# Keys' weights turned in two halves, and the first two token tiles together, at the start of a linear-attention and Mish block

## The chip, the cores and the metric

The kernel runs on one core of one Trainium2 chip. The time is the device time of one execution in microseconds; it is the median of several. Before the change it is 173.72 us, the median of three executions between 173.6 and 174.08.

A core has a matrix engine (TensorE, PE in the profile; its weight loads are the row PEld), an elementwise and reduction engine (VectorE, DVE), an engine for functions and copies (ScalarE, ACT), GpSimd (POOL) and SyncE (SP), which here only issues transfers. Engines run side by side, each works through its own instructions in order, and they wait for each other by semaphores. ACT can issue transfers too. All transfers run on the core's 16 DMA engines.

## The reference

With x of 2048 tokens by 512 (bf16), xn is x normalised over its 512 values. The result is x plus an attention branch of xn plus a dense branch of xn.

```python
qkv = x @ wqkv                      # 32 heads of 16: q, k, v
pq = einsum("bhsd,hdf->bhsf", q, w_phi)
pk = einsum("bhsd,hdf->bhsf", k, w_phi)
phi_q = concatenate([softmax(pq), softmax(-pq)], -1)
phi_k = concatenate([softmax(pk), softmax(-pk)], -1)
kv = einsum("bhsf,bhsd->bhfd", phi_k, v)
z  = einsum("bhsf->bhf", phi_k)
o  = einsum("bhqf,bhfd->bhqd", phi_q, kv) / (einsum("bhqf,bhf->bhq", phi_q, z) + 1e-6)
A  = o.reshape(B, S, D) @ wo
h  = xn @ w1 + b1                   # 512 -> 1792
B  = (h * tanh(softplus(h))) @ w2   # Mish, 1792 -> 512
out = x + A + B
```

## The kernel before

The 2048 tokens are 16 tiles of 128, in four groups of four. All of x, of the turned normalised tokens (`xnT`) and of the activations lies in the core's memory. The logits of keys and queries are not computed in two products: the 16 by 16 matrices `w_phi` of the heads are laid out as blocks on a diagonal (`Wbd`, made by `weights_by_block`, L524, from the loaded `wsrc` and a mask), and the columns of `wqkv` for the keys are multiplied by them once ("folded") to give `wkp`. For this fold TensorE needs the keys' weights turned, `wT`, with `wT[p, j, r]` = row r, column 128 j + p of the keys' part. `load_turned` (L143) fetches it with a transposing DMA on the sync queue. The fold has four steps, one for each 128 rows of the weights (`F0 0` to `F0 3`, L156); step kt reads the columns 128 kt to 128 kt + 127 of `wT`'s last dimension, so steps 0 and 1 read rows 0 to 255 and steps 2 and 3 the rest. Each is copied to `wkp` by `FD` (L165). The queries' weights go the same way later, by `load_queries`.

Tiles 0 and 1 of the first group start by a path of their own, a tile at a time: statistics on VectorE (`LS`, L170 and L172), the inverse root on GpSimd (`RS`, L176 and L177), normalising on VectorE (`AZ`, L181), four transpositions on TensorE (`TP`, L560), and a copy to `xnT` (`TC`, L565). Then come the first logits (`LP`, L209): for each of the four row blocks of `wkp`, tile 0 and then tile 1. The values of tile 0 follow (`V 0`, L194, with weights `wv`), then tiles 2 and 3, then the rest: hidden layer (`H`, L228), Mish on ACT (`M`, L239), softmaxes (`E`, `X`, `S`, `R`, `N`), sums over keys (`A`), second layer (`O`, L463), output projection (`P`, L470), residual (`Y`, L477).

The order of all this is written out by hand in `STEPS`: it is the order in which each engine gets its instructions. A step that waits holds up everything behind it on its engine. The transfers at the start are issued ahead of the steps, in the order of the code from L483: the sync queue issues tile 0 of x, `wT`, tiles 2 and 3, `wv`, the first half of `w1`, tiles 4 to 7, the second half of `w1`; ACT issues `wsrc`, tile 1 of x and the bias `b1b`. Transfers signal on eight semaphores in turn, so a later transfer also waits for an earlier one on the same semaphore. TensorE's first work is 12 matmuls on constants (L513), whose result nothing uses.

Of the kernel before, what the change touches and what calls it, by code (L numbers as in the profile page):

```python
# [21 lines left out]

WARM = 12
STEPS = """
LS 0; RS 0; DX 2; LS 1; WB; RS 1; AZ 0; TP 0 @0; F0 0 @1; F0 1 @2; AZ 1; FD 0 v; TP 1 @3; TC 1 v; LS
2; PB @4; RS 2; TC 0 a; LS 3; RS 3; FD 1 a; AZ 2; F0 2 @5; F0 3 @0; FD 2 a; FD 3 a; LP i @1,2; KM;
DX 3; AZ 3; V 0 @3; LC 0 0 a; TP 2 @5; V 1 @0; TC 2 a; TP 3 @1; VC 0 a; LC 0 1 v; TC 3 v; CB; L 0 2
@5; L 0 3 @2; LC 0 3 a; LN 1; H 0 @3; H 1 @1; H 2 @4; M 0; LC 0 2 a; H 3 @2; M 1; M 2; M 3; VC 1 a;
# [34 lines left out]
def kernel(  # L63
# [12 lines left out]
    nc = tc.nc  # L76
    P = 128
    S, D, NH, DH, F = 2048, 512, 32, 16, 1792
# [4 lines left out]
    FT = F // P  # L83
# [3 lines left out]
    x_v = A_x.flatten_outer_dims().rearrange("(t p) d -> p t d", p=P)  # L87
# [19 lines left out]
    x_sb = persist.tile([P, NT, D], BF16, name="x_sb")  # L107
# [29 lines left out]
            tables[0] = name  # L137
            nc.scalar.preload_act_table_set(name)  # L138

    def load_turned(base_col):  # L140

        wT = lnp.tile([P, 4, 512], BF16, name="wT", tag="xn")
        nc.sync.dma_start_transpose(out=wT[:], in_=A_wqkv[:, base_col : base_col + D])  # L143
        return wT

    def bank(b, name, dtype=FP32):
# [333 lines left out]

    part = (slice(0, 384), slice(384, 512))

    nc.sync.dma_start(x_sb[:, 0, :], x_v[:, 0, :])  # L483
    wT_of = {0: load_turned(D)}
    with nc.allow_non_contiguous_dma(reason="tiny w_phi load"):
        nc.scalar.dma_start(wsrc[:], wphi_v)
    nc.scalar.dma_start(x_sb[:, 1, :], x_v[:, 1, :])
    nc.scalar.dma_start(b1b[:], b1_v[:, :])
    nc.sync.dma_start(x_sb[:, 2:4, :], x_v[:, 2:4, :])
    nc.sync.dma_start(wv[:], wqkv_v[:, :, 2 * D : 3 * D])  # L490
# [8 lines left out]
    for sign in (1, -1):  # L499
        nc.gpsimd.affine_select(  # L500
            out=block[:], in_=block[:], pattern=[[-16 * sign, 8], [0, 16]],
# [83 lines left out]

    def load_weights(i):
        if i == 2:
            for f in (slice(0, 5), slice(5, 10), slice(10, FT)):
                nc.sync.dma_start(w2_sb[:, f, :], w2_v[:, f, :])
        else:  # L590
            nc.sync.dma_start(wo_sb, wo_v[:, :, :])
# [6 lines left out]
        pl_of[1, i] = project(wkp, TPG + i, wide_of[0][:, i - 1, :])  # L598

    def load_queries():  # L600
        wT_of[1] = load_turned(0)

    run = {
        "KM": masks, "WB": weights_by_block, "PB": bias,
# [2 lines left out]
        "LP": first_logits, "TC": lambda i, c: first_keep(i, copies[c]),  # L607
        "F0": lambda kt, b: fold(wT_of[0], kt, b), "FD": lambda kt, c: unfold(wkp, kt, copies[c]),
        "LN": stats, "AP": apply, "DX": load_tokens, "DW": load_weights, "WL": wide,
        "L": logits, "LC": lambda s, i, c: take(s, i, copies[c]),  # L610
        "V": value, "VC": lambda t, c: keep(t, copies[c]),
# [6 lines left out]
        "PH": lambda h: project_out(NT - 1, part[h]),  # L618
        "YH": lambda h: residual(NT - 1, part[h], (nc.scalar, nc.sync)[h]),
        "WT": load_queries,  # L620
        "F": lambda kt, b: fold(wT_of[1], kt, b), "FC": lambda kt, c: unfold(wqp, kt, copies[c]),
    }
# [33 lines left out]
```

## Time and profile before

| | |
|---|---|
| median of three executions | 173.72 us |
| the profiled execution, its own time | 174.0 us |
| its span in the profile | 172.3 us |
| granted TensorE clock in it | 1.0 |
| TensorE busy | 168.7 us, 98% |
| VectorE busy | 143.2 us, 83% |
| ACT busy | 119.5 us, 69% |
| bytes moved by DMA | 18.02 MB, 105 GB/s in the mean |
| from issue to landing: tile 0 of x, tile 1 of x, wT, tiles 2 and 3, wv | 2.4, 3.1, 5.4, 3.2, 4.5 us |

How to read it: times are from the start of the span. A line of the timeline has the start, the length, the engine, the line of the kernel, the operation, output and inputs, and in brackets how long the engine had been idle and what released it. SPq and ACTq are the two engines' queues issuing transfers: the length there is the time to issue, not to land. A group that the timeline merges has the length from its first start to its last end. A wait line has who waited for what, the total, the number of times and the longest, in us.

### The profile page before, as it was taken

The numbers are of one execution on the slowest core, as the hardware profiler recorded it, in microseconds if no ns is written. First come the engines' busy times: TensorE is split into PE (matmuls) and PEld (weight loads), VectorE is DVE, ScalarE is ACT, GpSimd is POOL, SyncE is SP. The second block draws the span as 40 slices with busy tenths as digits, with TensorE's granted clock in tenths as the row PEclk, the third lists the DMA queues.
The fourth block names the chain that finished last, engine by engine and source line by source line (L and its number), as shares of the span: only waits on it lengthen the run. The fifth ranks groups of instructions, "written<-read, shape, count | busy, mean of one in ns | idle before, by whom it ended". The sixth has DMA issues, their size and how long they took to land.

```text
span 172.3 us, 2713 instructions
## 1 busy us (share of the span) xinstructions
PE 168.7 (98%) x1039; PEld 82.4 (48%) x1039; DVE 143.2 (83%) x221; ACT 119.5 (69%) x192; POOL 9.4 (5%) x26
## 2 busy tenths in 40 slices
PE   8999999999999999999999999999999999999993
PEld 2554444444545444454446544444444545445452
DVE  2878998999997999979999999799988996844433
ACT  2446889979899998989999988974063883414200
POOL 4332205000000000000000000000000000000000
PEclk9999999999999999999999999999999999999999
DMA  5999350199930000000000363023974749885641
GB/s 98 269 377 365 82 98 0 37 189 207 366 120 0 0 4 0 0 0 0 4 0 0 64 118 66 12 51 67 150 152 93 150 95 144 172 168 100 173 134 61
DMA packets 44953, 18.02 MB, mean 105 GB/s; under 512 B 37004, under 2 KB 44940, under 8 KB 44940
## 3 DMA queue, kind: packets, MB, share of 16 engines
q1 hardware_dynamic: 44096, 17.60, 44.5%
q10 hardware_dynamic: 844, 0.25, 0.6%
q8 instruction: 8, 0.13, 0.3%
q14 instruction: 5, 0.04, 0.1%
HBM read 6.84 MB, written 2.10 MB: 52 GB/s over the span
## 4 chain that ended last, share of the span: by engine, by line
PE 95%; DMA 3%; SPq 0%; DVE 0%; issue 0%
PE po L463 28%; PE ph L228 28%; PE pl L194 14%; PE po L470 8%; PE pv L194 8%; DMA wT<-in_A_wqkv_dram 3%; PE pnd L418 2%; PE pkv L387 2%; PE pfold L156 1%; PE pwide L194 1%; PE pl L209 1%; PE ptr L560 0%; SPq L483 0%; DVE x_sb L477 0%; PE pb L533 0%
## 5 line engine op out<-in xcount | busy, mean ns | idle before, releaser
L463 PE MATMUL po<-w_sb,acts 128*128 128x512 bf16 (+2 forms) x238 | 50.7, 366 | 0.0
L228 PE MATMUL ph<-xnT,w_sb 128*128 128x512 bf16 x224 | 50.1, 379 | 0.0
L239 ACT ACTIVATE acts<-ph,b1f 128x512 bf16<-128x512 f32 x56 | 37.2, 694 | 4.6 <-PE ph L228 4.4
L305 DVE TENSOR_REDUCE s<-e 128x128 f32<-128x2048 bf16 x16 | 36.4, 2279 | 2.5 <-ACT e L288 2.5
L228 PEld LDWEIGHTS <-w_sb 128*128 128x128 bf16 x224 | 21.7, 98 | 25.5
L463 PEld LDWEIGHTS <-acts 128*128 128x128 bf16 x238 | 22.3, 98 | 24.1
L288 ACT ACTIVATE e<-e 128x2048 bf16<-128x2048 bf16 x16 | 30.3, 1908 | 0.0
L194 PEld LDWEIGHTS <-xnT 128*128 128x128 bf16 x184 | 17.6, 98 | 20.1 <-DMA wv<-in_A_wqkv_dram 0.2
L252 ACT CAST p_sb<-pl 128x512 bf16<-128x512 f32 x27 | 15.4, 587 | 5.5 <-PE pl L194 4.7
L433 ACT COPY ds<-pnd 128x32 f32<-128x32 f32 x16 | 2.9, 183 | 23.5 <-PE pnd L418 23.5
L194 PE MATMUL pv<-wv,xnT 128*128 128x512 bf16 x64 | 16.1, 379 | 0.0
L477 DVE TENSOR_TENSOR x_sb<-po,x_sb 128x512 bf16<-128x512 f32 (+2 forms) x17 | 10.9, 654 | 5.7 <-PE po L470 5.7
L470 PE MATMUL po<-wqk,xnT 128*128 128x512 bf16 (+2 forms) x68 | 15.5, 366 | 0.0
L194 PE MATMUL pl<-wqk,xnT 128*128 128x512 bf16 x64 | 15.3, 379 | 0.0
L170 DVE BATCH_NORM_STATS2 stats<-x_sb 128x6 f32<-128x512 bf16 x16 | 10.1, 679 | 4.3 <-DMA x_sb<-in_A_x_dram 4.3
L263 DVE TENSOR_TENSOR m<-m 128x512 bf16<-128x512 bf16 (+1 forms) x32 | 11.5, 358 | 1.1
L194 PE MATMUL pl<-wkp,xnT 128*128 128x512 bf16 x48 | 11.7, 379 | 0.0
L263 DVE TENSOR_TENSOR m<-p_sb 128x1024 bf16<-128x1024 bf16 x16 | 10.9, 682 | 0.2 <-ACT p_sb L252 0.2
L272 DVE TENSOR_TENSOR e<-p_sb,m 128x2048 bf16<-128x2048 bf16 x8 | 9.8, 1226 | 1.4 <-PE pkv L387 1.1
L272 DVE TENSOR_TENSOR e<-m,p_sb 128x2048 bf16<-128x2048 bf16 x8 | 9.8, 1225 | 0.3
L340 DVE TENSOR_TENSOR e<-e,r 128x2048 bf16<-128x2048 bf16 x8 | 9.6, 1215 | 0.0
L138 ACT ACT_TABLE_LOAD x7 | 9.0, 1283 | 0.1
(62 smaller groups left out, 131.4 us busy)
## 6 DMA issues: line engine op xcount, KB each, us to landing
out_dram<-x_sb SPq DMA_DIRECT2D x15, 128.0 KB, 2.0
w_sb<-in_B_w_dram SPq DMA_DIRECT2D x2, 896.0 KB, 7.8
x_sb<-in_A_x_dram SPq DMA_DIRECT2D x3, 512.0 KB, 10.0
w_sb<-in_B_w_dram SPq DMA_DIRECT2D x2, 640.0 KB, 8.8
wv<-in_A_wqkv_dram SPq DMA_DIRECT2D x1, 512.0 KB, 4.5
wqk<-in_A_wo_dram SPq DMA_DIRECT2D x1, 512.0 KB, 4.6
w_sb<-in_B_w_dram SPq DMA_DIRECT2D x1, 512.0 KB, 9.6
x_sb<-in_A_x_dram SPq DMA_DIRECT2D x1, 256.0 KB, 3.2
```

What stands on the lines that cost most here:

```text
L170: nc.vector.bn_stats(stats[:, i, :], xs[:, i, :])
L194: nc.tensor.matmul(pp, lhsT=xnT[:, t, kt, :], rhs=w[:, kt, :], start=(kt == 0), stop=(kt == KT - 1),)
L228: nc.tensor.matmul(ph_of[u][:], lhsT=w1_sb[:, kt, f * P : (f + 1) * P], rhs=xnT[:, g * TPG : (g + 1) * TPG, kt, :], start=(kt == 0), stop= ...
L239: nc.scalar.activation(acts[:, f, g * 512 : (g + 1) * 512], ph_of.pop(u)[:], ACT.Mish, bias=b1f[:, f : f + 1])
L252: copy(p_of[s][:, i, :], pl_of.pop((s, i)))
L263: nc.vector.tensor_tensor(out=m[:], in0=src[:, :, 0:half], in1=src[:, :, half : 2 * half], op=op)
L272: nc.vector.tensor_tensor(out=e_of[s][:].rearrange("p t j l c -> p (t j) l c")[:, :, pl, :].rearrange("p t (c e o) -> p t c e o", e=8, o=2 ...
L288: nc.scalar.activation(v, v, ACT.Exp)
L305: nc.vector.reduce_sum(t[:], pair(s, k).rearrange("p t j l (c e) -> p (t j l c) e", e=16), axis=AX.X)
L463: nc.tensor.matmul(po_of[t, c.stop][:, c], lhsT=acts[:, f, t * P : (t + 1) * P], rhs=w2_sb[:, f, c], start=(f == 0), stop=False,)
L470: nc.tensor.matmul(po_of[t, c.stop][:, c], lhsT=oT_of[t // 2][:, t % 2 * 4 + j, :], rhs=wo_sb[:, j, c], start=False, stop=(j == 3),)
L477: nc.vector.tensor_tensor(out=y, in0=po_of.pop((t, c.stop))[:, c], in1=y, op=ALU.add)
```

## The change

Tile 1 of x moves from ACT's queue to the sync queue, right behind tile 0 and ahead of `wT`. `wT` is fetched by two transposing DMAs of 256 rows each instead of one of 512; the queries' weights are still fetched by one. The step `WB`, which makes the block weights on VectorE, moves ahead of the statistics of tile 1. `w2` is loaded in two pieces of 7 blocks instead of three of 5, 5 and 4.

```diff
-LS 0; RS 0; DX 2; LS 1; WB; RS 1; AZ 0; TP 0 @0; F0 0 @1; F0 1 @2; AZ 1; FD 0 v; TP 1 @3; TC 1 v; LS
+LS 0; RS 0; DX 2; WB; LS 1; RS 1; AZ 0; TP 0 @0; F0 0 @1; F0 1 @2; AZ 1; FD 0 v; TP 1 @3; TC 1 v; LS
...
-    def load_turned(base_col):
+    def load_turned(base_col, *rows):
 
         wT = lnp.tile([P, 4, 512], BF16, name="wT", tag="xn")
-        nc.sync.dma_start_transpose(out=wT[:], in_=A_wqkv[:, base_col : base_col + D])
+        for r in rows:
+            nc.sync.dma_start_transpose(out=wT[:, :, r], in_=A_wqkv[r, base_col : base_col + D])
         return wT
...
-    nc.sync.dma_start(x_sb[:, 0, :], x_v[:, 0, :])
-    wT_of = {0: load_turned(D)}
+    for t in range(2):
+        nc.sync.dma_start(x_sb[:, t, :], x_v[:, t, :])
+    wT_of = {0: load_turned(D, slice(0, 256), slice(256, 512))}
     with nc.allow_non_contiguous_dma(reason="tiny w_phi load"):
         nc.scalar.dma_start(wsrc[:], wphi_v)
-    nc.scalar.dma_start(x_sb[:, 1, :], x_v[:, 1, :])
     nc.scalar.dma_start(b1b[:], b1_v[:, :])
...
-            for f in (slice(0, 5), slice(5, 10), slice(10, FT)):
+            for f in (slice(0, 7), slice(7, FT)):
                 nc.sync.dma_start(w2_sb[:, f, :], w2_v[:, f, :])
...
-        wT_of[1] = load_turned(0)
+        wT_of[1] = load_turned(0, slice(0, D))
```

## The prediction

> **What bounds the kernel now.** I read the page's busy shares first, then the chain that ended last in order of time, then the timeline of the first 12 us, then the waits and the landing times of the early transfers.
>
> The busy shares and the waits of TensorE's weight loads:
>
> ```profile
> PE 168.7 (98%) x1039; PEld 82.4 (48%) x1039; DVE 143.2 (83%) x221; ACT 119.5 (69%) x192; POOL 9.4 (5%) x26
> ...
> PEld L560 <- DVE xn L181: 0.8, 1, 0.8
> PEld L470 <- DMA xnT<-wv: 0.3, 1, 0.3
> PEld L156 <- DMA wT<-in_A_wqkv_dram: 0.3, 1, 0.3
> PEld L194 <- DMA wv<-in_A_wqkv_dram: 0.2, 1, 0.2
> ```
>
> TensorE is busy for 168.7 of 172.3 us. The 3.6 us left are 0.8 us ahead of the first matmul and about 2.6 us behind the last; in between it hardly stops. So this change can gain only by letting TensorE's stream start earlier, in the first 10 us, and it loses by every wait that it puts into that stream, since nothing later gives time back. The chain says the same: it starts with the keys' weights (1.25 to 6.61 us), passes the first logits, and is TensorE from there.
>
> ```profile
> 1.25 5.36 DMA wT<-in_A_wqkv_dram
> 8.16 1.73 PE pl L209 x8
> 9.88 0.86 PE pv L194 x4
> 10.97 0.86 PE pv L194 x4
> ```
>
> The timeline of those microseconds, with start and length first, carries the sum:
>
> ```profile
> 0.79 0.40 SPq L483 DMA_DIRECT2D x_sb<-in_A_x_dram  x1
> 0.83 5.28 PE L513 MATMUL warm<-const-bfloat16-1.0 128*128 128x512 bf16 x12 [0.83 <-PEq L640]
> 1.25 3.12 SPq L143 DMA_TRANSPOSE wT<-in_A_wqkv_dram  x1
> ...
> 4.41 0.69 DVE L170 BATCH_NORM_STATS2 stats<-x_sb 128x6 f32<-128x512 bf16 x1 [0.32 <-DMA x_sb<-in_A_x_dram]
> 4.42 0.56 SPq L489 DMA_DIRECT2D x_sb<-in_A_x_dram  x1
> 5.04 0.46 SPq L490 DMA_DIRECT2D wv<-in_A_wqkv_dram  x1
> 5.24 0.41 DVE L524 TENSOR_TENSOR Wbd<-block,wsrc 128x512 bf16<-128x512 bf16 x1
> 6.03 0.53 PE L560 MATMUL ptr<-ident,xn 128*128 128x128 bf16 x4
> 6.65 0.62 PE L156 MATMUL pfold<-Wbd,wT 128*128 128x128 bf16 x8
> 7.11 0.39 PE L560 MATMUL ptr<-ident,xn 128*128 128x128 bf16 x4
> 7.54 0.62 PE L156 MATMUL pfold<-Wbd,wT 128*128 128x128 bf16 x8
> 7.69 0.41 DVE L565 COPY xnT<-ptr 128x512 bf16<-128x512 bf16 x1
> 9.54 0.71 PEld L194 LDWEIGHTS <-xnT 128*128 128x128 bf16 x4 [0.15 <-DMA wv<-in_A_wqkv_dram]
> 9.72 1.03 PE L194 MATMUL pv<-wv,xnT 128*128 128x512 bf16 x4
> ```
>
> See three things. The first pair of folds waits for the whole of wT, but by only 0.27 us: TensorE is in its warm-up matmuls until 6.1 us anyway. Between that and the logits stands a second chain, on VectorE: statistics of tile 1, root on GpSimd, normalising (6.45), fold copy (7.08), copy of tile 1 turned (7.69 to 8.10), and the logits' second matmul follows at about 8.16. And the weights of the values, wv, land at 9.53, when the first value matmul wants to start: a third chain with almost no slack.
>
> **The change part by part.**
>
> Sync queue. Before, it issues x0 (0.40), wT whole (3.12), x2-3 (0.56), wv. After, it issues x0, x1, wT's first half, its second half, x2-3, wv. x1 adds one issue of 0.40 (x0's row) to 0.52 us (its own row on ACT's queue), so the first half starts at 1.25 + 0.45 = 1.70. What a transposition of 256 rows by 512 columns takes to issue, no row shows. Rows near: the 30 transpositions of as many elements (1024 by 128) take 1.23 to 1.32 us to issue in the medians of their three lines and land 3.2 to 3.6 us after their start, the slowest takes 2.47 to issue; the whole one took 3.12 here and 1.82 when repeated at 38.0 us with little else in flight. The 1.30 us between these last two I read as back-pressure: at 1.25 us x0, x1 and the small loads stand ahead in the DMA engines, which show a busy share of 0.98 from 2 to 3 us. Bounds for the two halves together: below 1.82 (the undisturbed whole), above 2.47 + 1.23 = 3.70 (the slowest and a usual one). I take 2.9, near the whole one's 3.12 less what x1, already issued, no longer shares, plus nothing for the second start. wT's issue then ends at 1.70 + 2.9 + 0.05 = 4.65, against 4.37: x2-3 and wv are issued 0.25 us later (ends: -0.8 and +1.1). Nearly all the DMAs of this phase are behind these: w1's first half lands at 11.9 and is wanted at 13.4, so 1.1 us are covered there; tokens 4 to 7 land at 13.4, where VectorE waits 0.83 for them, but what it makes of them (xnT 4 and 5, landed about 23.1) is wanted at 24.1. The waits on semaphores for a lane's earlier transfer, shifted by one transfer on this queue, fall on transfers that have long landed (x0, x1, wsrc, the first half).
>
> Landing of the halves. First: 1.70 + 3.2 = 4.9 (usual rows) to 1.70 + 5.36 = 7.1 (as late as the whole). Second: 4.9 + 1.3 = 6.2 to 7.1; I take 6.8, because the same bytes pass the same engines and x1's 128 KB go ahead. The second pair of folds wants it at about 7.4, so the second half is covered by 0.6 us. The first pair no longer waits: it starts behind the transposition of tile 0, which the warm-up bounds, at 6.03 + 0.43 = 6.46 instead of 6.65, a gain of 0.19 at that place.
>
> VectorE. WB (0.41, from 5.24) goes ahead of tile 1's statistics. It needs wsrc (landed 3.3) and starts at 4.10, behind tile 0's. So tile 1's statistics start at 4.10 + 0.35 (the row's pace; 0.41 at most) = 4.45 instead of 4.41, if x1 is there: issued at 1.25 and with x0's 2.4 to its own 3.1 us to landing, it comes at 3.7 to 4.35. Root and normalising of tile 1 shift by the same +0.04 to +0.10: normalised at 6.92 instead of 6.86. Tile 0's normalising moves from 5.57 to 5.4, behind the warm-up, so that gains nothing. The fold copy, which waited 0.22 for the fold, follows at once at 6.93 instead of 7.08; the turned copy of tile 1 ends at about 7.95 instead of 8.10. The logits gain 0.15 by this.
>
> ACT. One issue of 0.52 less ahead of the table load, which ends 2.8 us before ACT's first copy: no worth. Its three fold copies end at about 8.95 instead of 9.05, and the logits' last quarter wants them at 9.3: covered.
>
> Later loads of w2 in two pieces of 7 instead of 5, 5 and 4: issued around 40.5, wanted at 84.05 by the second layer; the cover is some 35 us, and one issue of about 0.5 us goes. Costed at nothing.
>
> The sum. The logits end 0.15 earlier, so the first value matmul could start at 9.57. wv, issued 0.25 later, lands at 9.53 + 0.25 = 9.78 if landing moves with issue, or at 9.53 if the engines' throughput sets it (share 0.9 to 1.1 from 7 us). I take 9.65; behind the landing come 0.05 to 0.18 us to the matmul: 9.8 instead of 9.72. The gain on the fold's wait is given back to wv: +0.1 us. On the profiled execution (span 172.3, its own time 174.0, 0.28 over the median 173.72) that is 174.1; on the median 173.8.
>
> A rule that speaks against the change: the halves write slices of wT whose column groups are no longer contiguous, while every transposition of this trace writes a whole tile. So slower halves are rival 2 below, with a price from this trace's own spread. The Trainium skill (DMA: Bandwidth & Descriptors, section Latency and other measured facts) says that a DMA transposition with a non-contiguous middle dimension loses about 30% of its bandwidth; no run here shows such a write. An estimate by that page is 1.4 times rival 2's transfer of 3.4 us, 1.4 us more, and a sum of about 174.7; by the rows it is 173.8.
>
> **The rivals.**
>
> 1. Slower: wv comes late because the two transpositions issue slowly. Price by the upper bound: issue of wT ends at 1.70 + 3.70 + 0.10 = 5.50, wv is issued 1.1 us later, lands at 10.6, and the first value matmul starts near 10.7, +1.0: 174.7. It decides (over 0.52 us) once wv lands after 10.15. For it: 2 of the later transpositions took 1.1 us more than the rest, and the first transposition is the slow one of its line. Against: an idle DMA queue would fetch wv faster than 4.5 us.
>
> 2. Slower: the halves themselves move slower because of their strided writes. Take the time from the end of x0's landing to wT's (3.18 to 6.61, 3.4 us) as wT's transfer. Transpositions of one line land 3.1 to 4.1 us after their start, a third apart; a third more is 1.1 us here, the second half lands at 7.9, the folds end at 8.4 instead of 8.0, and wv behind them in the same engines lands 0.5 to 1.1 later: +0.4 to +1.0, middle 174.4. Against: the number of elements and packets is the same.
>
> 3. Faster: the issues scale with size (1.82 for both), wv is issued 0.8 earlier and the DMA engines are clear sooner. Then the logits' chain is all that is left, and gives 0.15 to 0.2: 173.55, still inside the measurement. For more, TensorE's warm-up would have to end earlier too: its 12 matmuls go at 0.43 us each, twice the 0.216 of the logits, so an earlier switch of that pace would lay the wait for wT bare and make the halves worth up to 0.5 us more: 173.1.
>
> 4. The change does nothing: the halves land together, the first folds wait as before, wv moves by the 0.45 of x1 at most: 173.7 to 174.1.
>
> **How the numbers follow.** A measurement of this kernel tells about 0.3%, 0.52 us, from no change. The forecast (0.40) and rival 4 (0.10) and the small form of rival 3 (0.08) are within it: 0.58. Rival 1 has 0.17 and rival 2 has 0.12; together 0.29 slower. The larger form of rival 3 has 0.13. The likeliest, 173.8, is the prediction. The range takes in the small gain and most of both slower rivals: 173.35 to 174.75, with about 1 in 10 left on each side.
>
> **What would show it.** Right: two transpositions of 1.2 to 1.7 us each on the sync queue from 1.7 us, folds at about 6.46 without a wait for wT, WB near 4.1, tile 1's statistics at 4.45, the turned copy ending near 7.95, and a wait of TensorE's weight loads for wv of 0.2 to 0.4 us. Wrong: an issue of 2 us or more for one half, the second pair of folds waiting for wT beyond 7.6, the first value matmul after 10.2, or warm-up matmuls that end clearly before 6 us.

## The result, and the profile after

The changed kernel takes 174.59 us, the median of six executions (174.31 to 174.79), against 173.74 before: a ratio of 1.0047, 95% interval 1.0034 to 1.0061. It is slower by 0.85 us in the medians. The profiled execution is the fastest of the six, 174.31 us with a span of 172.6 us, so the profile shows less of the loss (0.31 us against the 174.0 of the profile before) than the medians do. A second profile of each kernel, below, closes most of that gap (0.52 us).

The changed kernel's page and its waits of TensorE's weight loads (total, times, longest, in us):

```profile
PE 168.1 (97%) x1039; PEld 82.1 (48%) x1039; DVE 143.1 (83%) x221; ACT 119.4 (69%) x192; POOL 9.5 (5%) x26
...
PEld L561 <- DVE xn L182: 1.3, 2, 0.8
PEld L195 <- DMA wv<-in_A_wqkv_dram: 0.9, 1, 0.9
PEld L471 <- DMA xnT<-wv: 0.4, 1, 0.4
```

The wait for wT (0.3 before) is gone; the wait for wv has grown from 0.2 to 0.9. The chain that ended last now leads through the sync queue's issues, those of wT's halves at L144 among them, to wv, and not through the landing of wT:

```profile
3.07 1.30 SPq L144
4.37 0.04 issue
4.41 0.58 SPq L490
4.99 0.05 issue
5.04 4.86 DMA wv<-in_A_wqkv_dram
9.89 0.05 issue
9.94 1.04 PE pv L195 x4
```

The changed kernel's timeline, with start and length first:

```profile
0.79 0.87 SPq L485 DMA_DIRECT2D x_sb<-in_A_x_dram  x2
0.82 4.46 PE L514 MATMUL warm<-const-bfloat16-1.0 128*128 128x512 bf16 x12 [0.82 <-PEq L641]
1.71 2.66 SPq L144 DMA_TRANSPOSE wT<-in_A_wqkv_dram  x2
...
3.93 0.41 DVE L525 TENSOR_TENSOR Wbd<-block,wsrc 128x512 bf16<-128x512 bf16 x1
4.26 0.68 DVE L171 BATCH_NORM_STATS2 stats<-x_sb 128x6 f32<-128x512 bf16 x1
...
5.04 0.46 SPq L491 DMA_DIRECT2D wv<-in_A_wqkv_dram  x1
...
5.84 0.62 PE L157 MATMUL pfold<-Wbd,wT 128*128 128x128 bf16 x8
...
6.79 0.40 PE L561 MATMUL ptr<-ident,xn 128*128 128x128 bf16 x4 [0.33 <-DVE xn L182]
...
7.25 0.41 DVE L566 COPY xnT<-ptr 128x512 bf16<-128x512 bf16 x1
...
7.69 1.89 PE L210 MATMUL pl<-wkp,xnT 128*128 128x512 bf16 x8
...
9.94 1.04 PE L195 MATMUL pv<-wv,xnT 128*128 128x512 bf16 x4 [0.36 <-DMA wv<-in_A_wqkv_dram]
```

Everything in front of wv came sooner: the folds at 5.84 instead of 6.65, the logits at 7.69 instead of 8.00. Not all of this is the change: the warm-up matmuls ended at 5.28 instead of 6.11 in this execution. TensorE then waits for wv, and the first value matmul is at 9.94 instead of 9.72. From there the two kernels run in step, 0.23 us apart to 160 us, with another 0.1 lost at the transposition ahead of the last output projections.

### The profile page after: what moved, and what is told of

It is laid out like the page before. It is cut to its first block, busy times and chain, and to the rows that moved or that the text cites. A ratio compares the mean times of both kernels' runs of the same rounds, so it can differ in the third digit from the quotient of the medians.

```text
span 172.6 us, 2712 instructions
## 1 busy us (share of the span) xinstructions
PE 168.1 (97%) x1039; PEld 82.1 (48%) x1039; DVE 143.1 (83%) x221; ACT 119.4 (69%) x192; POOL 9.5 (5%) x26
## 4 chain that ended last, share of the span: by engine, by line
PE 93%; DMA 3%; SPq 2%; issue 0%; DVE 0%
PE po L464 28%; PE ph L229 28%; PE pl L195 14%; PE pv L195 8%; PE po L471 8%; DMA wv<-in_A_wqkv_dram 3%; PE pnd L419 2%; PE pkv L388 2%; SPq L144 2%; PE pwide L195 1%; PE pfold L157 1%; SPq L485 0%; SPq L490 0%; PE ptr L561 0%; DVE x_sb L478 0%
## 5 line engine op out<-in xcount | busy, mean ns | idle before, releaser
L195 PEld LDWEIGHTS <-xnT 128*128 128x128 bf16 x184 | 17.5, 98 | 20.7 <-DMA wv<-in_A_wqkv_dram 0.9
L471 PEld LDWEIGHTS <-xnT 128*128 128x128 bf16 x68 | 6.1, 98 | 6.2 <-DMA xnT<-wv 0.4
```

The source lines that it names most:

```text
L195: nc.tensor.matmul(pp, lhsT=xnT[:, t, kt, :], rhs=w[:, kt, :], start=(kt == 0), stop=(kt == KT - 1),)
L471: nc.tensor.matmul(po_of[t, c.stop][:, c], lhsT=oT_of[t // 2][:, t % 2 * 4 + j, :], rhs=wo_sb[:, j, c], start=False, stop=(j == 3),)
```

## The experiments

Lines of diffs are those of the changed kernel unless said otherwise. Ratios are to the kernel before, on the same chip.

**The changed kernel again, and the kernel before again.** Unaltered, for a second profile each.

> The changed kernel once more, unaltered, for a second profile. Its first profiled execution took 174.31 us, the fastest of six whose median is 174.59; the wait for wv put the first value matmul at 9.94 us instead of 9.72. Theory (wv): the time beyond that is wv landing later still in other executions, so an execution of about 174.6 shows the first value matmul near 10.2 us and the same distance from there to the end. Rival (elsewhere): the first value matmul stays near 9.9 us and the rest is lost at a later place, at the transposition before the last output projections (0.4 us waited) or in the time outside the span.

> The kernel before, unaltered, for a second profile: its first profiled execution took 174.0 us, where the median is 173.8. Theory: the wait for wv is what differs between executions, so one near 173.7 shows the first value matmul 0.2 to 0.3 us sooner than 9.72, at 9.4 to 9.5. Rival: the first value matmul stays at 9.7 and the difference lies at the end.

The changed kernel: 174.39 us, ratio 1.0041 (1.0026 to 1.0056), its profile of an execution of 174.41. The kernel before: profile of an execution of 173.89. In both runs the theory (wv) held and its rival fell, at a first value matmul of 10.15 and 9.55. First the chain of the changed kernel, then the timeline of the kernel before:

```profile
5.05 5.05 DMA wv<-in_A_wqkv_dram
10.10 0.05 issue
10.15 1.04 PE pv L195 x4
```

```profile
1.25 2.67 SPq L143 DMA_TRANSPOSE wT<-in_A_wqkv_dram  x1
3.97 0.57 SPq L489 DMA_DIRECT2D x_sb<-in_A_x_dram  x1
4.58 0.47 SPq L490 DMA_DIRECT2D wv<-in_A_wqkv_dram  x1
...
9.55 1.03 PE L194 MATMUL pv<-wv,xnT 128*128 128x512 bf16 x4
```

In its second profile the kernel before issues the whole wT in 2.67 us, not 3.12, so wv goes out at 4.58 instead of 5.04 and no longer holds anything up: the first value matmul comes at the logits' pace, 9.55. The changed kernel issues wv at 5.04 to 5.05 in both and waits for it in both. The profile of before that the prediction started from was of an execution with a slow issue; the distance in a pair near the medians is 10.15 - 9.55 = 0.60 us, and not 0.22.

**One transposition again, tile 1 still on the sync queue.**

```diff
-    wT_of = {0: load_turned(D, slice(0, 256), slice(256, 512))}
+    wT_of = {0: load_turned(D, slice(0, 512))}
```

> The change with wT fetched in one transposition of 512 rows, all else as changed (tile 1 on the sync queue, WB early, w2 in two pieces). Theory (halves): the two transpositions keep the DMA engines longer than one, which pushes wv; undone, wv lands near 9.5 to 9.6 and the time is 173.7 to 173.9. Rival (place of tile 1): tile 1 ahead of wT on the same queue pushes wT and all behind it; then one transposition, issued 0.45 us later than before, gives wv at 9.9 or later and 174.4 to 174.9.

173.89 us, ratio 1.0008 (0.9999 to 1.0016): the loss is gone. The timeline:

```profile
1.71 2.38 SPq L144 DMA_TRANSPOSE wT<-in_A_wqkv_dram  x1
4.14 0.57 SPq L490 DMA_DIRECT2D x_sb<-in_A_x_dram  x1
4.76 0.46 SPq L491 DMA_DIRECT2D wv<-in_A_wqkv_dram  x1
...
6.38 0.62 PE L157 MATMUL pfold<-Wbd,wT 128*128 128x128 bf16 x8 [0.35 <-DMA wT<-in_A_wqkv_dram]
...
9.44 1.03 PE L195 MATMUL pv<-wv,xnT 128*128 128x512 bf16 x4
```

The folds wait for wT by 0.35 us here, which the halves avoid, and it costs nothing: the logits start at 7.72, as with the halves (7.69). The time that the halves save at the folds TensorE waits a little later for the normalised tile 1 (the 0.33 us at 6.79 in the changed kernel's first profile; here, with the folds later, no such wait is left). wv is issued 0.29 us earlier than with the halves and lands 4.2 us later, near 8.96, instead of 9.90 to 10.10. This rests on one profile.

**Two transpositions, tile 1 back on ACT's queue.** Run twice.

```diff
-    for t in range(2):
-        nc.sync.dma_start(x_sb[:, t, :], x_v[:, t, :])
+    nc.sync.dma_start(x_sb[:, 0, :], x_v[:, 0, :])
...
         nc.scalar.dma_start(wsrc[:], wphi_v)
+    nc.scalar.dma_start(x_sb[:, 1, :], x_v[:, 1, :])
```

> The change with tile 1 of x back on ACT's queue, wT in two transpositions. Theory (halves): no better than the change, 174.3 to 174.8, with wv landing at 9.8 or later although wT is issued 0.45 us earlier. Rival (place of tile 1): 173.5 to 173.8, wv near 9.5.

> The two transpositions with tile 1 back on ACT's queue, a second time for a second profile: the first was of an execution of 174.92 us where the median is 174.02. Theory: in a usual execution wv, issued near 4.73, lands at 9.3 to 9.6 and the first value matmul is at 9.5 to 9.7; the late landing at 10.6 is an outlier of the transfers. Rival: wv lands beyond 10 here too, and the median is lower for a reason behind the first 10 us.

174.02 us, ratio 1.0017 (0.9999 to 1.0036), and 173.89, ratio 1.0016 (0.9997 to 1.0035). My theory for the first of these runs, that nothing would come back, fell: undoing the place of tile 1 also takes most of the loss away. The second profile, of 173.78 us, is a usual execution:

```profile
1.25 2.67 SPq L144 DMA_TRANSPOSE wT<-in_A_wqkv_dram  x2
...
4.59 0.47 SPq L491 DMA_DIRECT2D wv<-in_A_wqkv_dram  x1
...
9.42 1.04 PE L195 MATMUL pv<-wv,xnT 128*128 128x512 bf16 x4
```

The first profile was of an execution of 174.92 us: wv, issued at 4.73, took 5.87 us and the first value matmul was at 10.65. Over both runs 4 of 24 executions are above 174.9; of the kernel before, beside them, none is above 174.31. So the two transpositions by themselves are not free in every execution.

So either part alone is nearly free by the medians (0.09 us and 0.07 to 0.22), and the two together are not (0.6 to 0.85). The intervals would still let the two transpositions alone cost up to 0.6 us. wv may land until about 9.4 us without a wait, since the logits hold the value matmul until 9.42 to 9.55 anyway. Tile 1 on the sync queue sends wv out 0.46 us later (5.05 against 4.59); with both parts it lands 4.9 to 5.2 us after its issue, in the profiles of this kernel and its variants below, where the whole wT behind tile 1 gave 4.2 (one profile). Beside tile 1 on ACT's queue the second transposition shows no such price in a usual execution: 4.8 us and an issue at 4.59, against 4.7 and 4.58 in the second profile of the kernel before. Each part alone fits into the slack that wv has in a usual execution, both together don't.

**The values of tiles 0 and 1 without wv.**

```diff
-        pv_of[t] = project(wv, t, bank(b, "pv")[:])
+        pv_of[t] = project(wkp if t < 2 else wv, t, bank(b, "pv")[:])
```

> The changed kernel with the values of tiles 0 and 1 computed from the folded keys' weights instead of wv, so that the first two value products do not wait for wv (those values are then other numbers; every instruction stays). Theory (wv): the logits' pace sets the first value matmul, 9.6 us, and the time is 0.35 us under the changed kernel at least, by the profile, and 0.6 to 0.9 by the medians: 173.7 to 174.0. Rival (elsewhere): the first products start earlier but the time stays within 0.2 of 174.6.

174.18 us, ratio 1.0020 (1.0011 to 1.0029): 0.2 to 0.4 us come back, less than expected. The first value matmul comes at 9.50, but its profile shows a wait behind it. That profile is of the slowest of the eleven executions (174.80):

```profile
PEld L195 <- DMA xnT<-xn: 1.3, 2, 1.0
...
PEld L229 <- DMA w_sb<-in_B_w_dram: 0.2, 1, 0.2
```

Tiles 4 to 7 landed at 15.06 in this execution (13.43 before, 13.83 in the changed kernel), so their statistics and their turning were late, and the values of tile 4 waited at 24.7 us. So a later load can take wv's place as what holds TensorE. In a usual execution of this kernel that is not shown: a first value matmul at 9.50 would give 173.8 by the table below, the median is 174.18, and the 0.3 us between them stay without a profile. The other profiles with both parts and two transpositions have tiles 4 to 7 at 13.83 to 14.16, and no wait at 24 us.

**Each half written to a contiguous place.** The queries' weights are fetched in two halves here too.

```diff
-        wT = lnp.tile([P, 4, 512], BF16, name="wT", tag="xn")
+        wT = lnp.tile([P, 2, 4, 256], BF16, name="wT", tag="xn")
-        for r in rows:
-            nc.sync.dma_start_transpose(out=wT[:, :, r], in_=A_wqkv[r, base_col : base_col + D])
+        for h in range(2):
+            nc.sync.dma_start_transpose(
+                out=wT[:, h], in_=A_wqkv[256 * h : 256 * h + 256, base_col : base_col + D]
+            )
...
-                lhsT=wT[:, j, kt * P : (kt + 1) * P],
+                lhsT=wT[:, kt // 2, j, kt % 2 * P : kt % 2 * P + P],
```

> The changed kernel with each half of wT written to a contiguous place of its own (the tile is laid out half by half; the queries' weights are fetched so too, in two halves). Theory (strided write): the halves are slow because each writes a slice with gaps; without the gaps the second half lands near 6.4 us as the whole one did, wv at 9.4 or before, and the time is 173.8 to 174.0. Rival (two transpositions): two of 256 rows keep the DMA engines longer than one of 512, however they write; then the second half lands at 6.9 to 7.2, wv at 9.8 to 10.2, and the time is 174.3 to 174.7.

174.45 us, ratio 1.0040 (1.0026 to 1.0055), the first value matmul at 10.27: as slow as the changed kernel, with no gap in the writes. The halves land 3.8 to 4.1 us after their issue, as they do there (3.8 and 4.1). My theory of the strided write, and with it rival 2 of the prediction, falls. The Trainium skill's loss of about 30% for a non-contiguous middle dimension (DMA: Bandwidth & Descriptors, section Latency and other measured facts) doesn't show here at the destination: the difference is within the intervals of the two. On the source side the rows have gaps in every version, and no run changes that.

**The same two transpositions cut by columns.**

```diff
-        for r in rows:
-            nc.sync.dma_start_transpose(out=wT[:, :, r], in_=A_wqkv[r, base_col : base_col + D])
+        for h in range(len(rows)):
+            n = 4 // len(rows)
+            nc.sync.dma_start_transpose(
+                out=wT[:, n * h : n * h + n],
+                in_=A_wqkv[:, base_col + n * h * P : base_col + (n * h + n) * P],
+            )
```

> The changed kernel with wT still in two transpositions of as many elements, but cut the other way: all 512 rows, 256 columns each, into a contiguous half of wT. The first folds then need both. Theory (per transposition): what a second transposition adds does not depend on how the weights are cut, so issues are 1.3 us each, wv is issued near 5.05 and lands at 9.8 to 10.2, and the time is 174.3 to 174.7. Rival (short rows): 256 rows make short pieces at the destination and these cost; with 512 rows the engines are done as early as with the whole, wv lands at 9.0 to 9.4 and the time is 173.8 to 174.1.

174.45 us, ratio 1.0037 (1.0024 to 1.0051), wv issued at 5.05 and landed at 10.09. How the weights are cut doesn't matter; that there are two transpositions does, behind tile 1 on the same queue.

**Four transpositions of 128 rows.**

```diff
-    wT_of = {0: load_turned(D, slice(0, 256), slice(256, 512))}
+    wT_of = {0: load_turned(D, *(slice(i, i + P) for i in range(0, D, P)))}
```

> The changed kernel with wT in four transpositions of 128 rows. Theory (two transpositions): each further transposition adds its own time; two more at the 0.6 to 0.8 us that one seems to add put the last landing at 8.2 to 8.8, wv at 10.9 to 11.7 and the time at 175.4 to 176.2. Rival (strided write): the number of gaps per written byte doubles but the number of transpositions does not matter by itself; wv moves by 0.3 us or less from the halves' 9.9 to 10.1 and the time stays at 174.3 to 174.9.

177.03 us, ratio 1.0183 (1.0169 to 1.0196), more than either expectation. The direction is that of a price for each transposition, but what makes it so large is the issue:

```profile
1.71 5.22 SPq L144 DMA_TRANSPOSE wT<-in_A_wqkv_dram  x4
6.98 0.58 SPq L490 DMA_DIRECT2D x_sb<-in_A_x_dram  x1
7.60 0.47 SPq L491 DMA_DIRECT2D wv<-in_A_wqkv_dram  x1
```

A transposition of 128 rows takes 1.26 to 1.29 us to issue, one of 256 rows 1.30 to 1.32. So four take 5.22 us, wv is issued 2.56 us later than in the changed kernel, and the DMA engines are idle half of the time meanwhile (busy shares of 0.28 to 0.59 from 4 to 8 us). The first value matmul is at 11.61. With two, the engines are not idle. The windows, of the changed kernel and then of the one with the whole wT (per stretch, behind the engines' busy times: granted clock, busy share of the DMA engines, GB/s; a share near or above 1 I read as engines that are never idle):

```profile
5.00:6.00 1.00, 0.69 (x9) 0.39 (x8) 0.54 (x2) 0.00 (x0) 0.76 (x3) 1.00 1.02 171
6.00:7.00 1.00, 0.67 (x12) 0.50 (x10) 0.68 (x2) 0.97 (x2) 0.28 (x1) 1.00 1.04 260
7.00:8.00 1.00, 1.00 (x15) 0.78 (x13) 0.76 (x3) 0.44 (x2) 0.00 (x0) 1.00 0.95 266
```

```profile
5.00:6.00 1.00, 0.48 (x5) 0.23 (x4) 0.56 (x2) 0.00 (x0) 0.76 (x3) 1.00 1.29 236
6.00:7.00 1.00, 0.65 (x13) 0.63 (x12) 0.60 (x2) 0.58 (x1) 0.32 (x1) 1.00 0.82 242
7.00:8.00 1.00, 1.00 (x15) 0.75 (x13) 1.00 (x3) 0.89 (x2) 0.00 (x0) 1.00 1.05 362
```

From 5 to 8 us the two halves' kernel moves 697 KB and the whole's 840, with the engines nearly as busy. The 143 KB are 0.4 us at the 380 to 390 GB/s of the microseconds that follow. The two transpositions don't do that by themselves: with tile 1 on ACT's queue the usual execution moved 820 KB in these three microseconds with two, and the kernel before 808 and 846 with one. Part of the 143 KB may come from the issues: tiles 2 and 3 and wv, which stand behind wT, go out 0.27 to 0.29 us later with the halves.

**The queries' weights in halves too.**

```diff
-        wT_of[1] = load_turned(0, slice(0, D))
+        wT_of[1] = load_turned(0, slice(0, 256), slice(256, 512))
```

> The changed kernel with the queries' weights, fetched at about 38 us with nothing else in flight, also in two transpositions of 256 rows: the halves measured by themselves. The whole one there lands 4.6 to 5.5 us after its start. If two halves cost more of themselves, the second lands 5.3 to 6.2 us after the first one's start; if they cost more only beside the other loads of the first microseconds, within 4.6 to 5.2. The time is that of the changed kernel, 174.2 to 174.7, since the folds of these weights come at 46 us.

One execution, 174.42 us. The first half is issued at 38.38, the second at 39.7, and they land 3.6 to 3.9 us after their own issue, so both are there 4.9 to 5.2 us after the first start. One whole transposition at this place took 4.3 to 5.5 us in the other profiles. With little else in flight the second transposition doesn't show in the landing of this one execution.

**WB and w2 undone.**

```diff
-LS 0; RS 0; DX 2; WB; LS 1; RS 1; AZ 0;
+LS 0; RS 0; DX 2; LS 1; WB; RS 1; AZ 0;
...
-            for f in (slice(0, 7), slice(7, FT)):
+            for f in (slice(0, 5), slice(5, 10), slice(10, FT)):
```

> The changed kernel with its two small parts undone: WB behind the statistics of tile 1 again, and w2 in three pieces again. Theory: neither carries any of the loss, 174.3 to 174.7, wv as in the changed kernel. Rival: WB ahead or the two larger pieces of w2 cost 0.3 us or more; then 174.1 or less.

174.51 us, ratio 1.0039 (1.0025 to 1.0052), the first value matmul at 10.10. Neither part carries any of it.

**The kernel before with wT ahead of everything** (diff against the kernel before):

```diff
-    nc.sync.dma_start(x_sb[:, 0, :], x_v[:, 0, :])
     wT_of = {0: load_turned(D)}
+    for t in range(2):
+        nc.scalar.dma_start(x_sb[:, t, :], x_v[:, t, :])
     with nc.allow_non_contiguous_dma(reason="tiny w_phi load"):
         nc.scalar.dma_start(wsrc[:], wphi_v)
-    nc.scalar.dma_start(x_sb[:, 1, :], x_v[:, 1, :])
```

> The kernel before with the whole wT first on the sync queue and both tiles of x on ACT's queue ahead of wsrc. wT is issued at 0.79 and lands near 6.0, wv is issued near 3.9 to 4.3 and lands at 8.5 to 9.0; tile 1's statistics start at 4.1 to 4.4 as before. Theory (the early chain sets the time): the first value matmul at 9.4, bound by the logits, and a time of 173.5 to 173.8. Rival (the end of the kernel sets it): no change from 173.8, as with the whole wT behind tile 1, where 0.1 us sooner at the start showed nothing at the end.

177.06 us, ratio 1.0159 (1.0119 to 1.0200). Both expectations fell. wT and wv did go out early, wv at 3.12, but the timeline of VectorE shows that tile 1 and wsrc came late:

```profile
3.12 0.69 DVE L170 BATCH_NORM_STATS2 stats<-x_sb 128x6 f32<-128x512 bf16 x1 [3.12 <-DMA x_sb<-in_A_x_dram]
...
6.05 0.69 DVE L170 BATCH_NORM_STATS2 stats<-x_sb 128x6 f32<-128x512 bf16 x1 [2.01 <-DMA x_sb<-in_A_x_dram]
...
7.17 0.43 DVE L524 TENSOR_TENSOR Wbd<-block,wsrc 128x512 bf16<-128x512 bf16 x1 [0.22 <-DMA wsrc<-in_A_w_phi_dram]
```

Tile 1, issued on ACT's queue at 1.19 us, landed at 6.05; wsrc, 16 KB, issued at 1.67, landed at 7.07. A second loss followed. TensorE had nothing to do for 2.54 us behind its warm-up, and when work came its granted clock had fallen to half:

```profile
7.98 0.60 PE L560 MATMUL ptr<-ident,xn 128*128 128x128 bf16 x4 [2.54 <-DVE xn L181]
```

```profile
8.00:9.00 1.00, 1.00 (x10) 1.00 (x11) 0.41 (x1) 0.39 (x1) 0.04 (x1) 0.52 1.09 357
9.00:10.00 1.00, 1.00 (x12) 0.78 (x10) 0.80 (x2) 0.73 (x2) 0.00 (x0) 0.50 1.04 376
...
11.00:12.00 1.00, 1.00 (x5) 0.39 (x4) 0.90 (x3) 0.63 (x2) 0.69 (x2) 0.78 1.10 359
```

The first value matmul came at 12.82. Of the six executions five had a mean granted clock of 0.99 and took 176.47 to 177.35 us, and the one at 1.0 took 174.83; so the late loads by themselves cost about 1 us in that one, and the rest goes with the clock (the profile, of one of the five, shows the fall). No version here beats the kernel before beyond its interval.

**What ties the runs together.** The place of the first value matmul goes with the time. In the profiles that have no other new wait in the first 30 us:

| profile | wv issued | landing after issue | first value matmul | time | difference |
|---|---|---|---|---|---|
| two halves, tile 1 on ACT, second | 4.59 | 4.8 | 9.42 | 173.78 | 164.36 |
| whole, tile 1 on sync | 4.76 | 4.2 | 9.44 | 173.88 | 164.44 |
| before, second | 4.58 | 4.7 | 9.55 | 173.89 | 164.34 |
| before, first | 5.04 | 4.5 | 9.72 | 174.00 | 164.28 |
| changed, first | 5.04 | 4.9 | 9.94 | 174.31 | 164.37 |
| queries' halves | 5.05 | 4.9 | 10.03 | 174.42 | 164.39 |
| WB and w2 undone | 5.04 | 5.0 | 10.10 | 174.50 | 164.40 |
| cut by columns | 5.05 | 5.0 | 10.13 | 174.45 | 164.32 |
| changed, second | 5.05 | 5.0 | 10.15 | 174.41 | 164.26 |
| contiguous halves | 5.04 | 5.2 | 10.27 | 174.67 | 164.40 |
| two halves, tile 1 on ACT, first | 4.73 | 5.9 | 10.65 | 174.92 | 164.27 |

The difference of time and first value matmul stays within 0.2 us over a range of 1.2. The kernel with wT ahead of everything fits too (177.12 and 12.82: 164.30). The one run that takes the wait for wv away gave back only a third to half of the loss, so the table shows what sets the time in these kernels and not that wv alone stands in the way.

## Why the prediction was right or wrong

The measured time lies inside the range, and wv was the right place to look. The likeliest case was wrong: 173.8 was forecast, within 0.3% of no change, and the kernel is 0.85 us slower in the medians. wv came late, as in rival 1, and at about its price (0.6 to 0.85 us of its 1.0), but not by rival 1's cause: the two transpositions did not issue slowly. That the time lies in the range is in part luck, since the upper end stood there for rivals 1 and 2, and the causes of both did not occur.

Right, step by step. The first folds no longer wait (5.84 and 6.30 in the two profiles; 6.46 forecast). WB runs at 3.93 behind tile 0's statistics (4.10), tile 1's statistics at 4.26 (4.45), the turned copy ends at 7.66 (7.95), and the logits gain 0.31 us in the first pair of profiles and 0.06 in the second (0.15). The halves are issued in 2.66 us (2.9), so wv goes out at 5.04 (5.29); a whole transposition took 2.67 in the second profile of before, so the halves cost nothing at the issue there. w2 and WB are worth nothing, as costed; the wait that grows is the one for wv, as the list of signs said, though to 0.9 and 1.0 us and not to 0.2 to 0.4. The logits' gain is worth nothing without wv, also as said.

Wrong, two terms of the sum for wv, and both towards a loss:

1. "x2-3 and wv are issued 0.25 us later" was worked out against a profile in which wT took 3.12 us to issue. That profile was 0.28 us above the median, and I carried the 0.28 along as a constant, on both sides alike. It was not constant: in the second profile of before wv goes out 0.46 us sooner, the first value matmul starts 0.17 sooner and the execution is 0.11 us shorter, so part of the 0.28 was this very issue. Against the second profile of before, wv goes out 0.46 us later, which is the one more issue on the queue. The row that should have warned was in view, the same transposition taking 1.82 us at 38 us.

2. "I take 9.65" for wv's landing assumed that landing moves with the issue or not at all. It moved by more: wv landed at 9.90 to 10.22, 4.9 to 5.2 us after its issue, where it was 4.5 and 4.7 in the kernel before, however the halves are cut or written. The sum has no term for this; with one transposition, or with tile 1 on ACT's queue, it was 4.2 and 4.8 in the usual executions.

Together they put the first value matmul at 9.94 to 10.15, against 9.8 forecast and 9.55 in a usual execution of before.

The cause that rival 2 names, strided writes, is refuted by the contiguous halves. Rival 3 didn't happen, since the issues of the halves don't scale with their size (1.30 to 1.32 us each, where 1.82 for both was its condition). The condition of its larger form did occur: in the first profile the warm-up ended at 5.28 us instead of 6.11 and the folds came at 5.84; it gained nothing, since wv waited behind. Rival 4 didn't happen: the halves land apart, at about 5.8 and 6.9 us in the first profile.

What stays open is why wv needs longer from issue to landing when tile 1 and two transpositions stand ahead of it on one queue. Behind tile 1 two pieces cost 143 KB of progress from 5 to 8 us against the whole in one profile; with tile 1 on ACT's queue, and beside little other traffic, the same two pieces show no delay in the usual executions. These are facts of these runs; the cause inside the engines is not shown. Open too is what holds the kernel in a usual execution once the wait for wv is gone.

## What to carry to other kernels

Cutting a transfer so that its first part arrives sooner pays only if its consumer is what ends last there, and it is paid by all that is queued behind: look for the next transfer on that queue whose landing has no slack. Two changes that each fit into one slack need not fit together, so undo them one at a time and both. Take a second profile of the kernel before where the first is off the median by as much as the effect: what makes it slow may be the thing that is changed.

## What the runs showed of the hardware that was not expected

- A DMA transposition of 256 rows of 512 took hardly longer to issue than one of 128 rows: 1.30 to 1.32 us and 1.26 to 1.29 in the changed kernel and the one with four; over all profiles 256 rows took 1.23 to 1.44. The whole 512 rows took 1.39 to 3.12.
- In the last experiment, with a whole transposition at the head of the sync queue, small loads on ACT's queue landed late: tile 1 took 4.9 us instead of 3.1, and 16 KB took 5.4 instead of 2.5. Tiles 2 and 3 and wv were issued on the sync queue meanwhile, at 2.23 and 3.12 us, so the transposition as the cause is not shown.
- In the same run 2.54 us without a matmul were followed by a granted clock of 0.50 to 0.52 for three microseconds; a gap of 0.82 us, in the kernel with four transpositions, left it at 1.0.
- The same 12 warm-up matmuls took 4.28 to 5.28 us together: where they took 5.28 single ones last 582 ns or more in the trace, and where they took less the last ones last 380 ns instead of 631. The granted clock reads 1.0 throughout.
